# A fused Mamba-2 scan and gated feed-forward: the first eight groups of TensorE work put in another order

## The chip, the core and the metric

The kernel runs on one core of a Trainium2 chip. The core has a matrix engine (TensorE, PE in the profile; PEld is its loading of weights), VectorE (DVE), ScalarE (ACT), GpSimd (POOL) and the DMA queues that SyncE (SP) starts. Each engine works through its own list of instructions in the order in which the program gives them, and waits for other engines by semaphores. TensorE writes its sums into PSUM, which VectorE and ScalarE read; GpSimd works in the main on-chip memory alone. The metric is the time of one execution on the device in microseconds (us), as the median of several runs.

## The reference, cut to what matters

Two stages follow each other. The first is a linear recurrence over 768 tokens for 4 sequences of 8 heads; it is done in chunks, with a matrix of decays inside a chunk and a state between chunks. The second takes the result as 3072 tokens of 256 numbers and sends it through two matrices with h * cos(h) between them.

```python
# x: (4, 8, 768, 32)   a: (4, 8, 768)   B, C: (4, 8, 768, 16)
cum = np.cumsum(log(clip(a)), axis=-1)                       # within a chunk
L = np.exp(cum[..., :, None] - cum[..., None, :]) * causal   # decay from token j to token i
y = (einsum('bhin,bhjn->bhij', C, B) * L) @ x                # inside the chunk
y += einsum('bhin,bhnd->bhid', C, state) * np.exp(cum)       # from the chunks before
state = exp(sum(la)) * state + sum_j(B_j x_j decay_from_j)

h = y @ w_in                 # y as (3072, 256), w_in (256, 2048)
out = (h * np.cos(h)) @ w_out   # w_out (2048, 256)
```

## The kernel before

The kernel uses chunks of 128 tokens, six in all. The first of them, chunk 0, is cut into two units of 64 tokens for all four sequences, so that the feed-forward can begin early. For each unit `k` it does the following. `spread_a` copies the decay factors to all partitions by a matrix product; `decays0` turns them into the matrix of decays with a scan on VectorE (each value is the one before times a factor, plus a start value). `turn_b` and `turn_c` transpose B and C. `inner` makes C times B (the tile g), `weights` multiplies it by the decays, and `finish0` makes y and the sums for the state.

The PSUM has three kinds of buffers here: tag `h` with two banks, tag `o` with two banks, and pairs of banks:

```python
def bank(shape, name, tag):
    return psum.tile(shape, FP32, tag=tag, bufs=2, name=name)

def pair(name):
    return psum.tile([P, 2, 4 * P], FP32, tag="scan", bufs=2, name=name)

def spread_a(k, p, i=0, n=1, tag="o"):
    ps = (pair("a_ps")[:, 0] if tag is None else bank([P, 4 * P], "a_ps", tag))
    ...                                       # two matmuls into ps

def decays0(k, p, i=0, n=1):                  # scan over half i of n, for pair p of sequences
    ...
    V.tensor_tensor_scan(out=lams[k][:, p, hs].rearrange(flat),
                         data0=spread.pop((k, p, i)).rearrange(flat), ...)

def inner(k, t):
    gs[k, t] = g = pair("g")
    ...                                       # 16 small matmuls into g

def weights(k, q):                            # reads gs[k, q] and lams[k], writes units[k]
    ...
    V.tensor_tensor(out=m, in0=gs[k, q][...], in1=l, op=ALU.mult)
```

`finish0` takes one pair for unit 0 and two pairs for unit 1. Its first pair holds a part of y and also the sums for the state; it hands back `take`, which reads these sums:

```python
def finish0(k, between=None):
    m, xk = units[k], xrs[k]
    y = [pair("y") for _ in range(2)] if k else [pair("y")]
    ...   # k == 1: from the state into y; both: the state's sums into y[0][:, s, 3 * P:]; then m times x into y
    if between:
        between()
    if k:
        for t in range(2):
            ACT.copy(out=t_[:, t]..., in_=y[t][:, :, 0:P])
    else:
        ACT.copy(out=t_..., in_=y[0][:, :, 0:2 * P]...)

    def take():
        for t in range(2):
            ts = slice(t * D, (t + 1) * D)
            ACT.activation(new[:, :, :, ts], y[0][:, :, 3 * P:]..., AF.Copy, scale=slot[:, t:t + 1])
    ...
    return take, add
```

A step `n` of the feed-forward is 256 of the 2048 inner columns for a group of 256 tokens. `first` makes hp, `wind` takes the whole turns off it (ScalarE makes k, VectorE makes w), `gate` is the sine on ScalarE, `gated` multiplies on VectorE and is the last that reads hp, and `second` is the product with w_out. In chunk 0 the even steps belong to unit 0 and the odd ones to unit 1; the steps 0 and 1 need the same columns of w_in, and so do 2 and 3.

```python
def first(n, between=None):
    c, f = divmod(n, NF)
    hp[n] = bank([P, TB], "hp", "h")
    ...
    for e in range(2):
        for k in range(KT):
            PE.matmul(to_[:, e], lhsT=w_in[:, k, fs], rhs=y[:, k], start=(k == 0), stop=(k == KT - 1), ...)
        if between and e == 0:
            between()

def wind_k(n): ACT.activation(k, hp[n], AF.Copy, bias=0.25, scale=INV_2PI)
def wind_w(n): V.scalar_tensor_tensor(out=w, in0=hp[n], scalar=INV_2PI, in1=k, op0=ALU.mult, op1=ALU.subtract)
def gate(n):   ACT.activation(cos, cos, AF.Sin, bias=quarter, scale=TWO_PI)
def gated(n):  V.tensor_tensor(out=gT[n], in0=hp.pop(n), in1=cos, op=ALU.mult)
```

The weights come as 64-bit words and are made into 32-bit numbers in eight pieces for each matrix: `grade` is two passes on ScalarE and a clip on GpSimd, `join` two passes on VectorE and an add on GpSimd.

Of the kernel before, what the change touches and what calls it, by code (L numbers as in the profile page):

```python
# [25 lines left out]
def kernel(  # L26
# [17 lines left out]
    P = 128  # L44
# [4 lines left out]
    TB = NB * P  # L49
# [19 lines left out]
    def bank(shape, name, tag):  # L69
        return psum.tile(shape, FP32, tag=tag, bufs=2, name=name)  # L70
# [279 lines left out]
    def decays0(k, p, i=0, n=1):  # L350

        if p == i == 0:
            lams[k] = scan.tile([P, 2, H, W], FP32, tag="lam", bufs=4, name="lam")
        flat = "p h i -> p (h i)"
        hs = slice(i * H // n, (i + 1) * H // n)
        V.tensor_tensor_scan(out=lams[k][:, p, hs].rearrange(flat),
                             data0=spread.pop((k, p, i)).rearrange(flat),
                             data1=unit0[:, hs].rearrange(flat), initial=0.0,
                             op0=ALU.mult, op1=ALU.add)
# [12 lines left out]
    def turn_c():  # L372

        tp = bank([P, 4, P], "tp", "o")
        for r in range(4):
            PE.transpose(tp[:, r], c0[:, r].rearrange("p h n -> p (h n)"), ident)
        tp = tp.rearrange("p r (b k g) -> p k b g r", b=NB, k=2)

        def of(k, dst, **v):
            ACT.activation(dst.rearrange("p b (g r) -> p b g r", r=4), tp[:, k], AF.Copy, **v)  # L380

        def take(k):
            for t in range(2):
                of(k, cuts[k][:, t].rearrange("p q (s i) -> p (q s) i", s=2), scale=slot[:, t:t + 1])
        return take, of

    def turn_b(k, tp):

        for p in range(2):
            PE.transpose(tp[:, 2 * k + p], bs[:, k, p], ident)  # L390
        return lambda: ACT.copy(out=bTs[:, k], in_=tp[:, 2 * k:2 * k + 2])
# [32 lines left out]
        V.tensor_tensor(out=m, in0=gs[k, q][:, :, 0:2 * P].rearrange("p k (s i) -> p k s i", s=2),  # L424
                        in1=l, op=ALU.mult)

    def finish0(k, between=None):

        m, xk = units[k], xrs[k]
        y = [pair("y") for _ in range(2)] if k else [pair("y")]  # L430
        at_ = [[(y[t][:, s, p * W:(p + 1) * W] if k else
                 y[0][:, s, t * P + p * W:t * P + (p + 1) * W]) for p in range(2)]
               for t in range(2) for s in range(2)]
        if k:
            old = states0.pop(k)
            for p in range(2):
                for s in range(2):
                    for q in range(4):
                        r, c0 = slice(32 * q, 32 * q + 32), W * (q % 2)
                        PE.matmul(at_[2 * (q // 2) + s][p][c0:c0 + W], lhsT=old[r, s, p],  # L440
                                  rhs=rTs[k][r, 2 * p + s], start=(p == 0), stop=False,
                                  tile_position=(32 * q, c0), skip_group_check=True)
        sc = scs.pop(k).rearrange("p (q k h) n -> p q k (h n)", q=2, h=2)
        x2 = xk.rearrange("p q (k h) d -> p q k (h d)", h=2)
        for p in range(2):
            for s in range(2):
                ss = slice(s * W, (s + 1) * W)
                for q in range(4):
                    PE.matmul(y[0][32 * q:32 * q + 32, s, 3 * P + p * W:3 * P + (p + 1) * W],
                              lhsT=sc[ss, p, q], rhs=x2[ss, p, q], start=(k == p == 0), stop=True,  # L450
                              tile_position=(s * W, 32 * q), skip_group_check=True)
        for p in range(2):
            for t in range(2):
                for s in range(2):
                    ss = slice(s * W, (s + 1) * W)
                    for q in range(4):
                        PE.matmul(at_[2 * t + s][p][32 * q:32 * q + 32],
                                  lhsT=xk[ss, p, 4 * t + q], rhs=m[ss, p, 4 * t + q],
                                  start=False, stop=True,
                                  tile_position=(s * W, 32 * q), skip_group_check=True)  # L460
        if k == 0:
            yT[0] = two.tile([P, 2, 2, 2 * P], FP32, tag="yT", name="yT")
        t_ = yT[0][:, k]
        if between:
            between()
        if k:
            for t in range(2):
                ACT.copy(out=t_[:, t].rearrange("p (s i) -> p s i", s=2), in_=y[t][:, :, 0:P])
        else:
            ACT.copy(out=t_.rearrange("p t (s i) -> p s t i", s=2),  # L470
                     in_=y[0][:, :, 0:2 * P].rearrange("p s (t i) -> p s t i", t=2))
        states0[k + 1] = new = states.tile([P, 2, 2, 2 * D], FP32, tag="state0", bufs=2,
                                           name="state0")
# [4 lines that stand above are left out]
                ACT.activation(new[:, :, :, ts], y[0][:, :, 3 * P:].rearrange(  # L478
                    "p s (q d) -> p s q d", q=2)[:, :, :, ts], AF.Copy, scale=slot[:, t:t + 1])

        def add():
            dec = scan.tile([P, 2, 2, 2 * D], FP32, tag="whole", bufs=1, name="whole")
            r4 = reach1.rearrange("p (q s) i -> p s q i", s=2)
            for s in range(2):
                G.tensor_tensor(out=dec[:, s], in0=old[:, s],
                                in1=r4[:, s, :, W:].to_broadcast([P, 2, 2 * D]), op=ALU.mult)
            G.tensor_tensor(out=new, in0=new, in1=dec, op=ALU.add)
            for u in range(2):
                state[0, u] = new[:, u].rearrange("p s (t d) -> p s t d", t=2)
        return take, add  # L490
# [158 lines left out]
        c, f = divmod(n, NF)  # L649
        return (f % 2, f // 2) if c == 0 else divmod(f, NJ)  # L650

    def first(n, between=None):
        c, f = divmod(n, NF)
        hp[n] = bank([P, TB], "hp", "h")

        u, j = turn_of(n)
        if c == 0:
            to_, y = hp[n].rearrange("p (e i) -> p e i", e=2), yT[0][:, u]
        else:
            to_ = hp[n].rearrange("p (e t s i) -> p e t s i", e=2, t=2, s=2)  # L660
            y = yT[c].rearrange("p k (u s t i) -> p k u t s i", u=2, s=2, t=2)[:, :, u]
        for e in range(2):
            fs = slice((2 * j + e) * P, (2 * j + e + 1) * P)
            for k in range(KT):
                PE.matmul(to_[:, e], lhsT=w_in[:, k, fs], rhs=y[:, k],  # L665
                          start=(k == 0), stop=(k == KT - 1), skip_group_check=True)
            if between and e == 0:
                between()
# [16 lines left out]
    def gate(n):  # L685
        cos = turns[n]
        ACT.activation(cos, cos, AF.Sin, bias=quarter, scale=TWO_PI)  # L687
# [146 lines left out]
        decays0(0, p, i, 2)  # L834
    spread_a(0, 1, 1, 2, "h")
    decays0(0, 1, 1, 2)
    take_c, of_c = turn_c()
    tp_b = bank([P, 4, P], "tp", "o")
    take_b = turn_b(0, tp_b)
    take_c(0)  # L840
    take_b()
    scan_reach = reach0(1)
    scan_reach()
    weigh0(0)
    grade("in", 0)
    for t in range(2):
        inner(0, t)
    spread_a(1, 0, tag="h")
    for q in range(2):
        weights(0, q)  # L850
    take_c(1)
    join("in", 0)
    weigh_c(1, of_c)
    take_s0, _ = finish0(0)
    spread_a(1, 1, tag="o")
    take_b = turn_b(1, tp_b)
    take_b()
    inner(1, 0)
    for p in range(2):
        decays0(1, p)  # L860

    la = const.tile([RB, NU, P], FP32, name="la")
    cut = const.tile([RB, NU, P], FP32, name="cut")
# [62 lines left out]

    def first_steps():

        take_s0()
        first(0, lambda: inner(1, 1))  # L930
        weigh0(1)
        grade("in", 1)
        units_of_decay()
        for q in range(2):
            weights(1, q)
        take_s1, add_s1 = finish0(1, lambda: wind_k(0))
        join("in", 1)
        wind_w(0)
        first(1)
        rest = grade("out", 0, later=True)  # L940
        gate(0)
        rest()
        clips()
        gated(0)
        join("out", 0)
        wind(1)
        first(2)
        rest = grade("in", 2, later=True)
        gate(1)
        take_s1()  # L950
        rest()
        gated(1)
        second(0)
        grade("out", 1)
        join("in", 2)
        wind(2)
        first(3)
        rest = grade("in", 3, later=True)
        gate(2)
        join("out", 1)  # L960
        rest()
        gated(2)
        second(1)
        wind(3)
        rest = grade("out", 2, later=True)
        gate(3)
        join("in", 3)
        rest()
        gated(3)
        return add_s1  # L970

    add_s1 = first_steps()
# [86 lines left out]
```

## Time and profile before

The time is 375.29 us, the median of three runs (375.26 to 376.05). The span of the profiled execution is 373.6 us.

| what | measured |
|---|---|
| full scans of unit 1 on VectorE | 1.21 us at 11.59, 1.22 us at 12.98 |
| scans of unit 0 in four halves | 2.44 us in all, from 5.09 |
| y of unit 1 on TensorE | 17.08 to 18.87 us |
| hp 0 complete | about 17.1 us |
| second(0) starts on TensorE | 23.97 us |
| sine of step 0 on ScalarE | 19.88 us, 0.74 us long |
| take_s1 on ScalarE | 23.74 us, 0.61 us for both parts |
| one step's k, w, sine, gT in the stage behind | 0.60, 0.68, 0.72, 0.68 us |

How to read the rows of such a profile: a row of the timeline has the start in us, the length in us, the engine, the line of the kernel, the operation, the tile that is written, an arrow, the tiles that are read, the form, and how many instructions were merged into the row. In square brackets stands how long the engine had been idle, and what ended the wait. Rows of one engine can overlap a little[...].

### The profile page before, as it was taken

Reading aid. Unit: us, or ns where it says so; the run is one execution under the profiler, and the core shown is the slowest. Engines: PE = TensorE matmul, PEld = TensorE weight load, DVE = VectorE, ACT = ScalarE, POOL = GpSimd, SP = SyncE. Lnnn points to the kernel's source line nnn. Section 1 sums busy time; section 2 is a strip of 40 time slices with the busy share of each in tenths; the row PEclk is TensorE's granted clock in tenths of the full one; section 3 lists DMA queues with packets and bytes.
Section 4 is the critical chain, followed back from the end, with each engine's and each line's share of the span. In section 5 each row is a group of like instructions: output and inputs, shape, how many; then the busy total and the mean of one; then the engine's idle time right before and its main releaser. Section 6 shows DMA issues by size and latency. Waiting matters only on the chain.

```text
span 373.6 us, 8681 instructions
## 1 busy us (share of the span) xinstructions
PE 363.9 (97%) x3272; PEld 325.2 (87%) x3272; DVE 280.8 (75%) x470; ACT 172.6 (46%) x293; POOL 215.2 (58%) x334
## 2 busy tenths in 40 slices
PE   7989999999999999999999999999999999999995
PEld 4568887889889899998999999899999989999995
DVE  6859999889699957987858987766987872543653
ACT  3487756444344435344434435434434443444442
POOL 6576865589856347664454683453685343544451
PEclk9999999999999999999999999999999999999999
DMA  9988987315436641755122735121020000010011
GB/s 142 270 230 239 254 212 155 86 14 139 121 84 84 124 108 17 112 128 135 21 51 28 130 94 138 18 50 17 10 37 7 21 9 2 2 28 2 5 26 28
DMA packets 121353, 31.54 MB, mean 84 GB/s; under 512 B 90496, under 2 KB 117216, under 8 KB 121312
## 3 DMA queue, kind: packets, MB, share of 16 engines
q1 hardware_dynamic: 119024, 30.54, 38.1%
q10 hardware_dynamic: 2288, 0.46, 0.7%
q8 instruction: 26, 0.43, 0.5%
q14 instruction: 15, 0.12, 0.1%
HBM read 27.64 MB, written 3.34 MB: 83 GB/s over the span
## 4 chain that ended last, share of the span: by engine, by line
PE 72%; DVE 11%; POOL 6%; DMA 3%; issue 3%; SPq 2%; ACT 1%; POOLq 0%; DVEq 0%; ACTq 0%
PE hp L665 35%; PE o L774 30%; POOL words L711 3%; DMA xr<-in_x_dram 3%; PE y L604 2%; DVE mag L246 2%; DVE gT L692 2%; DVE w L678 2%; PE g L562 2%; DVE mag L244 1%; DVE lam L512 1%; POOL gd L717 1%; PE y L597 1%; DVE m L583 1%; POOL gd L719 1%
## 5 line engine op out<-in xcount | busy, mean ns | idle before, releaser
L665 PE MATMUL hp<-yT,w_in 128*128 128x256 f32 x768 | 184.1, 382 | 2.5 <-DVE gT L692 1.5
L665 PEld LDWEIGHTS hp<-yT,w_in 128*128 128x128 f32 x768 | 139.2, 190 | 22.8 <-issue 4.7
L717 POOL TENSOR_TENSOR gd<-gT 128x256 f32<-128x256 f32 x79 | 59.2, 750 | 99.0 <-DVE gT L692 85.3
L687 ACT ACTIVATE w<-w,quarter 128x512 f32<-128x512 f32 x96 | 69.2, 721 | 77.1 <-DVE w L678 77.1
L672 ACT ACTIVATE k<-hp 128x512 int32<-128x512 f32 x96 | 57.1, 595 | 83.1 <-PE hp L665 82.9
L678 DVE SCALAR_TENSOR_TENSOR w<-hp,k 128x512 f32<-128x512 f32 x96 | 65.5, 682 | 38.3 <-ACT k L672 37.9
L692 DVE TENSOR_TENSOR gT<-hp,w 128x512 f32<-128x512 f32 x96 | 65.3, 680 | 35.9 <-ACT w L687 27.1
L774 PE MATMUL o<-words,gd 128*128 128x128 f32 x474 | 65.8, 275 | 0.0
L774 PEld LDWEIGHTS o<-words,gd 128*128 128x128 f32 x474 | 59.3, 192 | 0.0
L512 DVE TENSOR_TENSOR_SCAN lam<-arow,unit 128x512 f32<-128x512 f32 x40 | 56.6, 1415 | 0.0
L774 PEld LDWEIGHTS o<-w_out,gT 128*128 128x128 f32 x316 | 47.5, 191 | 4.0
L720 POOL TENSOR_TENSOR gd<-gT,gd 128x128 f32<-128x128 f32 x79 | 44.6, 565 | 6.2
L774 PE MATMUL o<-w_out,gT 128*128 128x128 f32 x316 | 48.0, 274 | 0.0
L719 POOL TENSOR_TENSOR gd<-gT,gd 128x128 f32<-128x128 f32 x79 | 44.2, 559 | 6.2
L583 DVE TENSOR_TENSOR m<-g,lam 128x256 f32<-128x256 f32 x80 | 30.9, 415 | 0.5
L774 PE MATMUL o<-w_out,gd 128*128 128x128 f32 x158 | 30.6, 275 | 0.0
L774 PE MATMUL o<-words,gT 128*128 128x128 f32 x158 | 30.6, 275 | 0.0
L736 PE MATMUL o<-w_out,gT 128*128 128x256 f32 x128 | 30.3, 380 | 0.0
L736 PEld LDWEIGHTS o<-w_out,gT 128*128 128x128 f32 x128 | 24.2, 190 | 3.4 <-POOL w_out L254 0.2
L774 PEld LDWEIGHTS o<-w_out,gd 128*128 128x128 f32 x158 | 24.0, 192 | 0.0
L774 PEld LDWEIGHTS o<-words,gT 128*128 128x128 f32 x158 | 24.0, 192 | 0.0
L791 DVE TENSOR_TENSOR sum<-ps,sum 128x256 f32<-128x256 f32 (+1 forms) x27 | 16.7, 645 | 0.6
(108 smaller groups left out, 264.4 us busy)
## 6 DMA issues: line engine op xcount, KB each, us to landing
arow<-a_cut SPq DMA_DIRECT2D x20, 512.0 KB
words<-in_moe_w_in_dram SPq DMA_DIRECT2D x8, 512.0 KB
words<-in_moe_w_out_dram SPq DMA_DIRECT2D x8, 512.0 KB
out_dram<-sum SPq DMA_DIRECT2D x18, 128.0 KB
blocks<-in_B_dram SPq DMA_DIRECT2D x128, 8.0 KB
blocks<-in_C_dram SPq DMA_DIRECT2D x128, 8.0 KB
xr<-in_x_dram SPq DMA_DIRECT2D x14, 128.0 KB
along<-a_all SPq DMA_DIRECT2D x20, 64.0 KB
```

The source lines that it names most:

```text
L512: V.tensor_tensor_scan(out=lam[c, b][:, hs].rearrange("p h i -> p (h i)"), data0=rows_.rearrange("p h i -> p (h i)"), data1=unit[:, b % 2 ...
L583: V.tensor_tensor(out=m_[js, :, :, is_], in0=g_[js, :, :, is_], in1=l_[js, :, :, is_], op=ALU.mult)
L665: PE.matmul(to_[:, e], lhsT=w_in[:, k, fs], rhs=y[:, k], start=(k == 0), stop=(k == KT - 1), skip_group_check=True)
L672: ACT.activation(k, hp[n], AF.Copy, bias=0.25, scale=INV_2PI)
L678: V.scalar_tensor_tensor(out=w, in0=hp[n], scalar=INV_2PI, in1=k, op0=ALU.mult, op1=ALU.subtract)
L687: ACT.activation(cos, cos, AF.Sin, bias=quarter, scale=TWO_PI)
L692: V.tensor_tensor(out=gT[n], in0=hp.pop(n), in1=cos, op=ALU.mult)
L717: G.tensor_tensor(out=d[:, 0:2], in0=g[:, 1:2].to_broadcast([P, 2, P]), in1=g[:, 3::-3], op=ALU.subtract)
L719: G.tensor_tensor(out=d[:, 2], in0=g[:, 0], in1=d[:, 0], op=ALU.subtract)
L720: G.tensor_tensor(out=d[:, 3], in0=g[:, 2], in1=d[:, 2], op=ALU.subtract)
L736: PE.matmul(o[c, u][:, t], lhsT=g[:, 2 * e + t], rhs=w_out[:, 2 * j + e], start=(j == e == t == 0), stop=(j == NJ - 1 and e == 1), skip_gr ...
L774: PE.matmul(at[q], lhsT=a_[q], rhs=w[q], start=(j == 0 and q in starts), stop=(j == NJ - 1), skip_group_check=True)
```

## The change

The change puts the work of chunk 0 into another order; the arithmetic stays the same. The first half of unit 1's decays is scanned in two halves, straight behind the scans of unit 0, where VectorE waits for the first g; the scan for the reach (how much of the state is left at each token) moves back behind the rest. Both halves of `inner` of unit 1 come ahead of hp 0, and `finish0(1)` goes into hp 0, between its two halves. The steps 2 and 3 take their hp from the pairs in place of tag `h`, and come ahead of `second(0)`; `second(0)` and `second(1)` move back. `take_s1` moves from behind `gate(1)` to behind `gate(3)`. `clips` (the decays of the later chunks) goes ahead of `gate(0)`, and `join` goes ahead of `gated` in the steps 0 and 1. It is meant to keep TensorE fed over the first steps, in which the hp banks and the waits for y hold it up.

```diff
@@ -424,7 +424,7 @@
         V.tensor_tensor(out=m, in0=gs[k, q][:, :, 0:2 * P].rearrange("p k (s i) -> p k s i", s=2),
                         in1=l, op=ALU.mult)
 
-    def finish0(k, between=None):
+    def finish0(k):
 
         m, xk = units[k], xrs[k]
         y = [pair("y") for _ in range(2)] if k else [pair("y")]
@@ -461,8 +461,6 @@
         if k == 0:
             yT[0] = two.tile([P, 2, 2, 2 * P], FP32, tag="yT", name="yT")
         t_ = yT[0][:, k]
-        if between:
-            between()
         if k:
             for t in range(2):
                 ACT.copy(out=t_[:, t].rearrange("p (s i) -> p s i", s=2), in_=y[t][:, :, 0:P])
@@ -649,9 +647,9 @@
         c, f = divmod(n, NF)
         return (f % 2, f // 2) if c == 0 else divmod(f, NJ)
 
-    def first(n, between=None):
+    def first(n, between=None, tag="h"):
         c, f = divmod(n, NF)
-        hp[n] = bank([P, TB], "hp", "h")
+        hp[n] = bank([P, TB], "hp", tag) if tag else pair("hp")[:, 0]
 
         u, j = turn_of(n)
         if c == 0:
@@ -834,30 +832,34 @@
         decays0(0, p, i, 2)
     spread_a(0, 1, 1, 2, "h")
     decays0(0, 1, 1, 2)
+    spread_a(1, 0, 0, 2, None)
+    decays0(1, 0, 0, 2)
     take_c, of_c = turn_c()
     tp_b = bank([P, 4, P], "tp", "o")
     take_b = turn_b(0, tp_b)
+    spread_a(1, 0, 1, 2, "h")
+    decays0(1, 0, 1, 2)
     take_c(0)
     take_b()
-    scan_reach = reach0(1)
-    scan_reach()
     weigh0(0)
     grade("in", 0)
     for t in range(2):
         inner(0, t)
-    spread_a(1, 0, tag="h")
+    spread_a(1, 1, tag="h")
     for q in range(2):
         weights(0, q)
     take_c(1)
     join("in", 0)
+    decays0(1, 1)
+    take_s0, _ = finish0(0)
+    take_b = turn_b(1, tp_b)
+    scan_reach = reach0(1)
+    scan_reach()
+    take_b()
+    take_s0()
+    for t in range(2):
+        inner(1, t)
     weigh_c(1, of_c)
-    take_s0, _ = finish0(0)
-    spread_a(1, 1, tag="o")
-    take_b = turn_b(1, tp_b)
-    take_b()
-    inner(1, 0)
-    for p in range(2):
-        decays0(1, p)
 
     la = const.tile([RB, NU, P], FP32, name="la")
     cut = const.tile([RB, NU, P], FP32, name="cut")
@@ -926,47 +928,47 @@
 
     def first_steps():
 
-        take_s0()
-        first(0, lambda: inner(1, 1))
         weigh0(1)
         grade("in", 1)
         units_of_decay()
         for q in range(2):
             weights(1, q)
-        take_s1, add_s1 = finish0(1, lambda: wind_k(0))
+        states_of = []
+        first(0, lambda: states_of.extend(finish0(1)))
+        take_s1, add_s1 = states_of
         join("in", 1)
-        wind_w(0)
+        wind(0)
         first(1)
         rest = grade("out", 0, later=True)
+        clips()
         gate(0)
         rest()
-        clips()
+        join("out", 0)
         gated(0)
-        join("out", 0)
+        first(2, tag=None)
         wind(1)
-        first(2)
         rest = grade("in", 2, later=True)
         gate(1)
+        rest()
+        join("in", 2)
+        gated(1)
+        first(3, tag=None)
+        wind(2)
+        rest = grade("out", 1, later=True)
+        gate(2)
+        rest()
+        join("out", 1)
+        second(0)
+        gated(2)
+        wind(3)
+        second(1)
+        rest = grade("in", 3, later=True)
+        gate(3)
         take_s1()
         rest()
-        gated(1)
-        second(0)
-        grade("out", 1)
-        join("in", 2)
-        wind(2)
-        first(3)
-        rest = grade("in", 3, later=True)
-        gate(2)
-        join("out", 1)
-        rest()
-        gated(2)
-        second(1)
-        wind(3)
-        rest = grade("out", 2, later=True)
-        gate(3)
         join("in", 3)
-        rest()
         gated(3)
+        grade("out", 2)
         return add_s1
 
     add_s1 = first_steps()
```

## The prediction

> **What bounds the kernel now.** I read the page first (engine shares, slices, chain), then the PE timeline of the first 31 us with what PE waited for, then VectorE over the same stretch, and last the busy shares of the stage behind it.
>
> ```profile
> PE 363.9 (97%) x3272; PEld 325.2 (87%) x3272; DVE 280.8 (75%) x470; ACT 172.6 (46%) x293; POOL 215.2 (58%) x334
> ...
> PE   7989999999999999999999999999999999999995
> ...
> DVE  6859999889699957987858987766987872543653
> ...
> PEclk9999999999999999999999999999999999999999
> ...
> PE hp L665 35%; PE o L774 30%; POOL words L711 3%; DMA xr<-in_x_dram 3%; PE y L604 2%; DVE mag L246 2%; DVE gT L692 2%; DVE w L678 2%; PE g L562 2%; DVE mag L244 1%; DVE lam L512 1%; POOL gd L717 1%; PE y L597 1%; DVE m L583 1%; POOL gd L719 1%
> ```
>
> PE is full from the first slices on. The whole idle time of PE is 373.6 - 363.9 = 9.7 us, so a change in the head can bring very little; it can lose more, because nothing behind it has slack to take a delay back.
>
> ```profile
> 13.76 0.67 PE L415 MATMUL g<-cT,turned 32*64 32x128 f32 x16 [0.46 <-ACT turned L391]
> 14.36 1.13 PE L665 MATMUL hp<-yT,w_in 128*128 128x256 f32 x4
> 15.42 0.67 PE L415 MATMUL g<-cT,turned 32*64 32x128 f32 x16
> 16.02 1.13 PE L665 MATMUL hp<-yT,w_in 128*128 128x256 f32 x4
> 17.08 0.69 PE L440 MATMUL y<-rT,state 32*64 32x64 f32 x32
> ...
> 19.20 1.99 PE L665 MATMUL hp<-yT,w_in 128*128 128x256 f32 x8 [0.33 <-ACT yT L468]
> 21.49 1.32 PE L665 MATMUL hp<-yT,w_in 128*128 128x256 f32 x5 [0.30 <-DVE gT L692]
> ...
> 25.77 1.89 PE L665 MATMUL hp<-yT,w_in 128*128 128x256 f32 x8
> ```
>
> These are the steps to be moved: g of unit 1 in two halves around half of hp 0, y of unit 1 at 17.08, hp 1 at 19.20, hp 2 at 21.49 (it waits for gated(0), which frees its bank), hp 3 at 25.77. Full groups of eight follow each other at 1.73 us from 29.54 on (33.07, 34.80, 36.52), which is 0.216 us for one pass of 256 columns.
>
> ```profile
> 8.16 0.70 DVE L398 TENSOR_TENSOR_SCAN m<-a_ps,m 128x260 f32<-128x260 f32 x1 [0.64 <-PE a_ps L396]
> 9.32 1.29 DVE L424 TENSOR_TENSOR m<-g,lam 128x512 f32<-128x512 f32 x2 [0.46 <-PE g L415]
> ...
> 16.15 0.69 DVE L424 TENSOR_TENSOR m<-g,lam 128x512 f32<-128x512 f32 x1 [0.96 <-PE g L415]
> ...
> 20.65 0.69 DVE L692 TENSOR_TENSOR gT<-hp,w 128x512 f32<-128x512 f32 x1 [2.15 <-ACT w L687]
> ...
> 28.72 0.68 DVE L692 TENSOR_TENSOR gT<-hp,w 128x512 f32<-128x512 f32 x1
> ```
>
> VectorE's gap is the one around 8.16; gT 0 ends at 21.3, gT 2 only at 29.4. Then the stage that follows:
>
> ```profile
> 29.50:53.90 24.40, 24.36 (x113) 21.24 (x113) 23.79 (x32) 16.63 (x29) 18.32 (x19) 1.00 0.89 248
> ```
>
> Columns: length, then busy time of PE, PEld, DVE, ACT, POOL. PE and VectorE are both full (24.36 and 23.79 of 24.40 us). A PE that is ahead at 29.5 us would meet VectorE; a PE that is behind takes VectorE with it, since each step's w waits for its hp.
>
> ```profile
> 1.06 2.93 PE L84 MATMUL warm<-ones 128*128 128x512 f32 x4 [1.06 <-DVE quarter L277]
> 3.92 2.34 PE L346 MATMUL a_ps<-m,those 128*64 128x256 f32 x16
> ```
>
> **What the Trainium skill says.** "TensorE: Matmul & The Clock Gate", section "HAM oscillation": no PE gaps of over about 3.4 us, or PE falls back to half its clock. The trace shows the cold half: the warm-up has two passes of 512 and two of 256 columns, 2 x 0.432 + 2 x 0.216 = 1.30 us at the later pace, and took 2.93; the granted-clock row doesn't show it. "PSUM — Partial Sum Buffer", section "Specifications (TRN2)": eight banks of 2 KiB, 512 FP32 each. The kernel spends all eight: tag h two, tag o two, and two pair tiles of two banks. Section "Engine vs sequencer instructions" there: ScalarE, VectorE and GpSimd are strict FIFO. The traces agree: the rows on each engine follow the program's order. So I place the instructions of each engine in the new program order and carry durations over from the rows.
>
> **Part 1: the first scan of unit 1 earlier.** Removed: two full scans of 1.21 us at 11.59 and 12.98. Added: two halves of about 0.61 us at 7.5 and 8.6, one full scan behind join("in", 0); the reach scan (0.70) goes from 8.16 to behind that. VectorE has about 1.7 us between scan end (7.5) and weights(0) (9.32), and two halves are 1.2, so weights(0) moves by 0.1 us at most, and finish0(0) waits for x at 10.82 anyway. VectorE: join to 11.7, full scan to 12.9, reach to 13.55. PE no longer has spread_a(1,1) (1.08 us at 11.85) behind y 0: turn_b and reach by about 12.9. ACT: yT 0 to 12.6, take_b to 12.92, take_s0 to 13.5. So g of unit 1: first half 12.97 to 13.64, second (its pair is released by take_s0) 13.6 to 14.27; weights(1) 13.7 to 15.0, against 16.84 before: 1.8 us won here.
>
> **Part 2: y of unit 1 inside hp 0.** Half of hp 0 at 14.05 (0.87 us of issue), y from 15.05 (it needs weights(1) for its second pair), as long as before, 17.08 to 18.87 = 1.79, so to 16.84; the other half of hp 0 16.7 to 17.6 lies under the yT copies (ACT 16.9 to 17.55). hp 1 from 17.6 instead of 19.20: 1.6 us earlier. The price: hp 0 is complete at 17.75 instead of 17.1, so k 0 runs 17.8 to 18.4 (was 17.18), w 0 to 19.1, sine to 19.85. join("out", 0) and clips now come ahead of gated(0): gT 0 at 20.75 against 20.65.
>
> **Part 3: hp 2 and hp 3 in pair tiles.** hp 2 needs no gated(0) any more: a pair is free after the second yT copy (17.5), w_in's piece 1 is added by 18.35; so it runs 19.33 to 21.1, against 21.49 to 24.1. For hp 3 I read which pairs are live. There are two. y[0] of unit 1 also holds the sums for the state, which take_s1 reads, and take_s1 is moved behind gate(3). gate(3) needs hp 3. So y[0]'s pair can't be hp 3's, the only other pair is hp 2's, and hp 3 must wait until gated(2) has read hp 2. That hp 3 uses only one bank of a pair doesn't help, if a tile is given back as a whole.
>
> When is gated(2)? ACT, VectorE and GpSimd make it, in program order:
> - GpSimd: clip of out 0 19.0 to 19.6, clips to 20.65, add of out 0 20.85 to 22.1 (1.27), clip of in 2 to 22.75.
> - VectorE: gT 0 to 21.35, w 1 to 21.95, join("in", 2) 22.8 to 24.0, gT 1 to 24.65, w 2 to 25.2.
> - ACT: k 1 20.4, sine 1 22.0 to 22.7, k 2 23.25 to 23.85, sine 2 25.25 to 25.95.
> - GpSimd: add of in 2 24.05 to 25.3, clip of out 1 to 25.95; VectorE join("out", 1) 26.0 to 27.2, gT 2 27.2 to 27.9 (before 28.72 to 29.4).
>
> So hp 3 starts at 27.95, and second(0) and second(1) stand behind it in PE's order: PE stands still from 21.1 to 27.95, 6.85 us. Then four groups at 1.73: hp 3, second(0), second(1), hp 4 end at 34.9, plus 0.25 until the last sum is there; w 4 then starts about 35.7 on VectorE (k 4 is 0.6) against 32.17 before: +3.5 us. An idle time of 6.85 us is also long enough for the half clock; the warm-up lost 2.93 - 1.30 = 1.6 us to it, and I take the same: +1.6. Sum +5.1 at 30 to 37 us, and since PE and VectorE are both full behind it, all of it reaches the end: 375.3 + 5.1 = 380.4. I take 0.2 off for short waits that a later stage may swallow: 380.2.
>
> **Rivals.** (A) hp 3 has its bank after all (half a pair is enough, or y[0] comes free by other means). Then hp 3 runs 21.1 to 22.9, second(0) to 24.6, second(1) after gT 1 to 26.4, hp 4 to 28.2, where before it started at 29.54. But ACT, VectorE and GpSimd keep their chain: gT 2 27.9, then w 3, join("in", 3) behind the add of out 1, gT 3 31.1, w 4 at 31.0 to 31.7 against 32.17. VectorE is full until 58 us, where hp already waits 0.4 us for gT, so only VectorE's 0.5 to 1.1 us counts: about 374.4. For it speaks the name of the change, which means both banks to be used; against it the place of take_s1. I give it 15%. (B) The stall is there but PE stays warm or is cold only briefly: +3.5, 378.8; against it, the idle time is far over the skill's 3.4 us and the start shows the cold pace. (C) The moves of parts 1 and 2 come to nothing because x or the words arrive late: x of unit 1 is needed at 15.6 instead of 17.7. The row for in 1 shows its words there by 14.12, and x of unit 1 is the next in the queue, so at most some tenths. In all three the rest of the program is the same; only the head's shift differs.
>
> **Range and chances.** With the stall (85%) the time lies between 378 and 382.5, by how long the half clock lasts (none to 3 us) and by errors of half a microsecond in the chain to gated(2); without it about 374.4. The range 376.0 to 382.5 leaves out the second and the worst tail. 2% is 7.5 us: faster than 367.8 would need almost all of PE's idle time, 1%; slower than 382.8 needs a long cold stretch, 8%; within 2%: 91%.
>
> **What would show it.** In the trace after: (1) a full-width scan fewer at 12 to 14 us, two half scans at 7.5 to 9.3, weights(0) still at 9.3 to 9.4; (2) both g halves by 14.3, y of unit 1 near 15.1, hp 1 near 17.6; (3) hp 2 near 19.3 without a wait for gT; (4) hp 3 with the one long wait of PE, 6 to 7 us, put down to VectorE's gT, and its passes near 0.43 instead of 0.216 us; (5) from 40 us on the same rows, about 5 us later. Wrong would be: hp 3 close behind hp 2 (then rival A), or a long wait with passes at 0.216 us (rival B).

## The result and the profile after

The changed kernel takes 381.91 us (median of four runs, 381.57 to 382.39) against 375.29 us. The ratio is 1.0173, with a 95% interval of 1.0154 to 1.0191: 6.6 us slower.

From the page of the changed kernel, in the order of the lines shown of the kernel before: busy times, the slices, and the chain of waits by line.

```profile
PE 366.1 (96%) x3276; PEld 327.9 (86%) x3276; DVE 280.3 (74%) x471; ACT 172.6 (45%) x293; POOL 215.0 (56%) x334
...
PE   8929999999999999999999999999999999999996
...
DVE  7672899989979966987775887875888782554543
...
PEclk9996999999999999999999999999999999999999
...
PE hp L663 37%; PE o L772 30%; SPq L110 4%; PE y L602 3%; PE o L734 2%; PE g L560 2%; POOL words L709 2%; DMA bc<-in_C_dram 1%; PE y L595 1%; DMA arow<-a_cut 1%; DVE mag L246 1%; DVE gT L690 1%; DVE w L676 1%; DVE mag L244 1%; POOL gd L715 1%
```

The span is 380.6 us, 7.0 longer. There are two marks of it: the third slice of PE (19 to 28.5 us) has a 2 where the kernel before has an 8, and the slice behind it (28.5 to 38 us) was granted 6 tenths of the clock. PE's busy time is 2.2 us longer although the work is the same (3276 matmuls in place of 3272, since one spread is cut in halves): it has slow passes, shown below.

The PE timeline of the changed kernel, the same steps as before:

```profile
12.49 1.19 PE L415 MATMUL g<-cT,turned 32*64 32x128 f32 x32 [0.17 <-ACT turned L391]
13.61 1.13 PE L663 MATMUL hp<-yT,w_in 128*128 128x256 f32 x4
14.67 0.45 PE L440 MATMUL y<-rT,state 32*64 32x64 f32 x14
15.58 0.50 PE L440 MATMUL y<-rT,state 32*64 32x64 f32 x18 [0.45 <-issue]
...
17.11 3.07 PE L663 MATMUL hp<-yT,w_in 128*128 128x256 f32 x13
21.99 1.67 PE L663 MATMUL hp<-yT,w_in 128*128 128x256 f32 x7 [1.80 <-issue]
28.82 3.75 PE L663 MATMUL hp<-yT,w_in 128*128 128x256 f32 x8 [5.16 <-DVE gT L690]
32.37 4.85 PE L734 MATMUL o<-w_out,gT 128*128 128x256 f32 x16
37.05 1.89 PE L663 MATMUL hp<-yT,w_in 128*128 128x256 f32 x8
```

The row at 17.11 holds the second half of hp 0 (4 passes), all of hp 1 (8) and the first pass of hp 2. The row at 28.82 is hp 3. It waited 5.16 us, and the profile names gT on VectorE as what ended the wait. Its 8 passes take until second(0) starts at 32.37, 3.55 us in place of 1.73, and the two groups behind it take 4.68 in place of 3.46. hp 4 starts at 37.05; before, it started at 29.54.

VectorE in the changed kernel: weights(0), weights(1), gT 2, w 3, w 4.

```profile
9.12 1.29 DVE L424 TENSOR_TENSOR m<-g,lam 128x512 f32<-128x512 f32 x2 [0.39 <-PE g L415]
...
13.22 1.29 DVE L424 TENSOR_TENSOR m<-g,lam 128x512 f32<-128x512 f32 x2
...
27.99 0.68 DVE L690 TENSOR_TENSOR gT<-hp,w 128x512 f32<-128x512 f32 x1
33.30 0.69 DVE L676 SCALAR_TENSOR_TENSOR w<-hp,k 128x512 f32<-128x512 f32 x1 [4.63 <-ACT k L670]
...
39.61 0.69 DVE L676 SCALAR_TENSOR_TENSOR w<-hp,k 128x512 f32<-128x512 f32 x1 [3.29 <-ACT k L670]
```

gT 2 ends at 28.67 and hp 3 starts at 28.82. In the kernel before, w 4 stood at 32.17; here it is at 39.61, 7.4 us later, after two long waits of VectorE for PE. The busy shares by stages of the changed kernel (length; busy PE, PEld, DVE, ACT, POOL; granted clock; DMA share; GB/s):

```profile
25.00:30.00 5.00, 1.18 (x3) 1.03 (x4) 2.81 (x5) 1.27 (x2) 3.11 (x3) 0.80 0.75 181
30.00:35.00 5.00, 5.00 (x14) 3.96 (x13) 1.12 (x2) 2.13 (x5) 0.61 (x1) 0.51 1.07 305
35.00:40.00 5.00, 5.00 (x25) 4.41 (x24) 1.68 (x3) 2.98 (x6) 1.86 (x2) 1.00 0.58 138
```

In the first stretch every engine stands for a good part: PE is busy for 1.18 of 5 us, VectorE for 2.81. In the next PE is "busy" for 5.00 of 5 us but does 14 passes where 24 or 25 are usual, at a granted clock of 0.51.

### The profile page after: what moved, and what is told of

The parts are those of the page before. It is cut to its first block, busy times and chain, and to the rows that moved or that the text cites. A ratio compares the mean times of both kernels' runs of the same rounds, so it can differ in the third digit from the quotient of the medians.

```text
span 380.6 us, 8692 instructions
## 1 busy us (share of the span) xinstructions
PE 366.1 (96%) x3276; PEld 327.9 (86%) x3276; DVE 280.3 (74%) x471; ACT 172.6 (45%) x293; POOL 215.0 (56%) x334
## 4 chain that ended last, share of the span: by engine, by line
PE 78%; SPq 5%; DVE 5%; POOL 5%; DMA 3%; issue 2%; ACT 1%; POOLq 0%; ACTq 0%
PE hp L663 37%; PE o L772 30%; SPq L110 4%; PE y L602 3%; PE o L734 2%; PE g L560 2%; POOL words L709 2%; DMA bc<-in_C_dram 1%; PE y L595 1%; DMA arow<-a_cut 1%; DVE mag L246 1%; DVE gT L690 1%; DVE w L676 1%; DVE mag L244 1%; POOL gd L715 1%
## 5 line engine op out<-in xcount | busy, mean ns | idle before, releaser
L772 PEld LDWEIGHTS o<-w_out,gT 128*128 128x128 f32 x316 | 47.5, 191 | 4.0
L734 PE MATMUL o<-w_out,gT 128*128 128x256 f32 x128 | 31.3, 390 | 0.0
L734 PEld LDWEIGHTS o<-w_out,gT 128*128 128x128 f32 x128 | 25.3, 198 | 3.7
L232 POOL TENSOR_SCALAR mag<-mag 128x512 f32<-128x512 f32 x16 | 11.6, 726 | 11.1 <-ACT mag L231 11.0
```

The costliest lines, as they stand in the source:

```text
L734: PE.matmul(o[c, u][:, t], lhsT=g[:, 2 * e + t], rhs=w_out[:, 2 * j + e], start=(j == e == t == 0), stop=(j == NJ - 1 and e == 1), skip_gr ...
L772: PE.matmul(at[q], lhsT=a_[q], rhs=w[q], start=(j == 0 and q in starts), stop=(j == NJ - 1), skip_group_check=True)
```

## The experiments

My theory: y[0] of unit 1 keeps its pair until take_s1; hp 3 therefore gets the pair of hp 2 and has to wait for gated(2); PE cools in that wait. All edits are against the changed kernel unless the text says otherwise. The kernel before ran beside each group of runs: 375.37 us beside runs 1 to 4, 375.5 beside runs 6 to 9, 375.14 beside runs 5, 10 and 11.

### 1. hp 3 in a bank of tag h

```diff
-        first(3, tag=None)
+        first(3)
```

> Only hp of step 3 goes back to a bank of tag h. Theory (the pair of y[0] is held by take_s1, so hp 3 must wait for gated(2), and PE cools meanwhile): hp 3 follows hp 2 at about 23.7 us with no long wait, its passes stay at 0.216 us, hp 4 starts near 28.8 and the time is 374.3 to 375.3, some 7 us under the changed kernel. Rival 1 (the loss comes from unit 1's new order or from the joins ahead of gated): the time stays at 380 to 382. Rival 2 (second(0) and second(1) come too late, whatever bank hp 3 has): 378 to 380.

Measured: 375.88 us, ratio to the kernel before 1.001 (0.9998 to 1.0022). The PE timeline of this run:

```profile
16.99 3.07 PE L663 MATMUL hp<-yT,w_in 128*128 128x256 f32 x13
21.85 3.40 PE L663 MATMUL hp<-yT,w_in 128*128 128x256 f32 x15 [1.79 <-issue]
25.09 3.62 PE L734 MATMUL o<-w_out,gT 128*128 128x256 f32 x16
28.54 1.89 PE L663 MATMUL hp<-yT,w_in 128*128 128x256 f32 x8
```

hp 3 follows hp 2 in one row, at 0.216 us for a pass. One word in one line takes the whole loss away, so both rivals fall. The time is 0.6 us above the span I gave; runs 8 to 11 are about that.

### 2. hp 3 in a pair, take_s1 early

```diff
         take_s1, add_s1 = states_of
+        take_s1()
...
         gate(3)
-        take_s1()
```

> hp 3 stays in a pair, but take_s1 comes straight behind the copies of y of unit 1. Theory: y[0]'s pair is free at about 18.4 us, hp 3 takes it without a wait, and the time is that of the run with hp 3 in tag h within 0.5 us (374.3 to 375.5). If a pair is held for another reason than take_s1, hp 3 still waits for gT 2 at about 28.8 and the time is 381 to 382.

Measured: 375.8 us, ratio 1.0009 (0.9993 to 1.0024), the same as run 1. hp 2 and hp 3 again run in one row, 21.98 to 25.38. So a pair serves hp 3 as well as a bank of tag h does, and the place of take_s1 alone decides whether it is free.

### 3. The wait left in, PE kept at work

```diff
+        fill(bank([P, 4, P], "warm", "o"), 5)
         first(3, tag=None)
```

> The wait of hp 3 stays; five products of ones with 512 columns each, into a free bank, fill 4.3 us of it, so that PE doesn't stand idle for 5.2 us. Theory (the slow passes of hp 3 and second(0) come from the idle time): the passes of hp 3 are at 0.216 us, hp 3 and second(0) take 3.46 us in place of about 6.5, and the time is 3 us under the changed kernel, 378.5 to 379.3. If the half clock has another cause, the time stays at 381.5 to 382.3.

Measured: 379.65 us, ratio 1.0111 (1.0077 to 1.0146). The fills (`warm` in the rows) only write a bank that is free at the time. Its PE timeline:

```profile
23.70 4.46 PE L84 MATMUL warm<-ones 128*128 128x512 f32 x10
29.04 1.97 PE L663 MATMUL hp<-yT,w_in 128*128 128x256 f32 x8 [0.88 <-DVE gT L690]
30.84 3.62 PE L734 MATMUL o<-w_out,gT 128*128 128x256 f32 x16
34.30 1.89 PE L663 MATMUL hp<-yT,w_in 128*128 128x256 f32 x8
```

hp 3 still waits for gT 2 and starts 0.2 us later than in the changed kernel, but hp 4 starts at 34.30 in place of 37.05. From hp 3 to hp 4 it is 5.26 us here and 8.23 (37.05 - 28.82) there. The idle time thus costs 2.97 us of slow passes on top of the wait itself; in the medians the difference is 2.3 us (381.91 - 379.65), under the 3 us I gave, and the time lies 0.35 above the span of 378.5 to 379.3.

### 4. and 5. Each part alone

Run 4 keeps unit 1's new order and gives the steps 0 to 3 their old order and banks. Run 5 is the kernel before with only the steps 0 to 3 as changed.

```diff
# run 4, the core of it
-        first(2, tag=None)
+        first(2)
...
-        first(3, tag=None)
+        second(0)
+        grade("out", 1)
...
+        first(3)
```

> Unit 1's new order (scans, g, y inside hp 0) with the old order of the steps 0 to 3 and their banks. Theory: no long wait; hp 1 ends 0.8 us earlier than before, but k 0 is 1.1 us later than before, and hp 2 waits for gT 0; the time is 374.5 to 376.0, near the kernel before. Rival 1 (unit 1's new order makes the loss): 379 to 382.

```diff
# run 5, against the kernel before, the core of it
+        first(2, tag=None)
...
-        first(2)
...
+        first(3, tag=None)
...
-        second(0)
-        grade("out", 1)
...
-        first(3)
```

> The complement: unit 1 in the old order, and only the steps 0 to 3 as changed (hp 2 and hp 3 in pairs, take_s1 behind gate(3), joins ahead of gated). Theory (the whole loss is in the bank of hp 3): hp 3 waits 4 to 6 us for gT 2, passes at half pace behind it, time 381.0 to 383.0. Rival (the loss needs unit 1's new order too): under 379.

Measured: run 4 375.69 us, ratio 1.0013 (0.9995 to 1.0031); run 5 381.79 us, ratio 1.0176 (1.0163 to 1.0189). The PE timeline of run 5:

```profile
28.70 3.75 PE L665 MATMUL hp<-yT,w_in 128*128 128x256 f32 x8 [5.20 <-DVE gT L692]
32.25 4.86 PE L736 MATMUL o<-w_out,gT 128*128 128x256 f32 x16
36.95 1.89 PE L665 MATMUL hp<-yT,w_in 128*128 128x256 f32 x8
```

These are the rows of the changed kernel at 28.82, 32.37 and 37.05 within 0.12 us. The steps' part makes the whole loss; unit 1's part makes no difference that can be told from none.

### 6. and 7. What is the gap in hp 2?

The wait of 1.80 us at 20.2 to 22 us is put down to "issue". Counted from the first matmul on, it stands behind 347 records (a record is one matmul in the trace) in both kernels. Run 6 starts two loads of weights later, run 7 cuts the warm-up into more and shorter matmuls; both have hp 3 in tag h. Each was executed once.

```diff
# run 6
-    for w in (("in", 2), ("out", 1), ("in", 3), ("out", 2), ("in", 4)):
+    for w in (("in", 2), ("out", 1), ("in", 3)):
...      # at the end of clips()
+        for w in (("out", 2), ("in", 4)):
+            fetch(*w)
```

> Hp of step 3 in tag h, and two of the 512 KB loads of weights (out 2 and in 4) start only behind the clips, at about 21.5 us. The gap of PE at 20.1 to 21.9 us, which the profile puts down to issue, comes behind the same 347th matmul record in the kernel before, in the changed one and in three of the four runs. Theory (it waits for its next block of instructions, and that transfer stands behind the loads of the weights): with 1 MB less in the queues before 21 us the gap falls from 1.8 us to under 1.0. Rival (the fetch takes its 6 us whatever else moves): the gap stays at 1.6 to 1.9.

```diff
# run 7
-    fill(bank([P, 4, P], "warm", "o"), 1)
-    fill(bank([P, 2, P], "warm", "o"), 1)
+    for blocks_ in (4, 2):
+        warm = bank([P, blocks_, P], "warm", "o")
+        for i in range(blocks_):
+            fill(warm[:, i:i + 1])
```

> Hp of step 3 in tag h, and the two warm-up products cut into six of 128 columns, which is 8 matmul records more ahead of everything else with the same columns. Theory (a block of instructions ends there): the gap stays behind the 347th record, which is now the first pass of hp 1 instead of the first of hp 2, and the gap on y moves by 8 records as well. Rival (something that hp 2 needs comes late, w_in's piece 1 or its bank): the gap stays in front of hp 2's second pass.

PE in run 6, then PE in run 7:

```profile
22.16 5.08 PE L663 MATMUL hp<-yT,w_in 128*128 128x256 f32 x15 [2.06 <-issue]
```

```profile
17.38 1.56 PE L663 MATMUL hp<-yT,w_in 128*128 128x256 f32 x6
22.57 6.70 PE L663 MATMUL hp<-yT,w_in 128*128 128x256 f32 x22 [3.63 <-issue]
```

Run 7: with 8 records more at the head the gap comes 7 passes sooner (behind 6 passes of hp, not 13), which is behind 348 recorded matmuls. The gap on y, which was to move as well, is not seen in run 7. The gap here is 1.8 us longer and ends at 22.57, where that of run 1 ends at 21.85. So it belongs to a count of instructions and to a time, not to hp 2 or to what hp 2 reads. A matmul record goes with one weight load; the gap of 0.45 us on y in the changed kernel stands behind 220 records, and 347 - 220 = 127 pairs are 254 instructions. The Trainium skill, "Runtime: NRT & Kernel Launch", section "Instruction fetch mechanics", says that an engine refills its instruction memory in blocks of 16 KiB, 256 instructions, "mostly hidden". The block fits; "hidden" doesn't hold here, where the gap in hp was 0.3 to 3.6 us.

The traces also have the transfer itself. Of 19 to 20 us in the changed kernel:

```profile
q8 instruction: 1, 0.02, 6.9%
```

This is one packet of 16 KB in the instruction queue, in flight from 19.58 to 20.69 us; the gap ends at 21.99. The whole execution has 26 such packets. At 256 instructions each, as that page has it, they hold 6656 (an estimate); PE ran 6552 matmuls and weight loads, and no other engine more than 471 instructions. In all 13 profiles the second of these packets lands between 20.50 and 21.91 us, and the gap ends 1.2 to 1.5 us behind its landing (run 7: 21.17 and 22.57; run 11: 21.05 and 22.48). The first lands at 14.29 in the changed kernel, and the gap on y ends at 15.58. So the gap is a wait for the next block of instructions; what takes the 1.2 to 1.5 us behind the landing is not shown.

Run 6 missed: the gap stayed at 2.06 us. DMA traffic in 15 to 20 us fell only from 376 GB/s (run 1) to 319, and the packet started no sooner (19.83, in run 1 19.39). From 20 to 22 us it fell to under 50 GB/s, and the packet took 1.07 us all the same, 1.11 in run 1. What decides when it starts is not shown. Its time of 379.73 us, and 378.16 us in run 7, are each of one execution and are not compared; 15 passes after run 6's gap took 4.92 us (22.16 to 27.08) where run 1 took 3.24.

### 8. to 11. Why is nothing gained when the stall is gone?

In run 1 hp 4 starts at 28.54, 1.0 us sooner than before, and the time is no better. Four runs look for that microsecond; all have hp 3 in tag h. Run 8 moves take_s1 and the grading of out 2 on ScalarE. Run 9 grades and joins each piece a step earlier (in 1 is piece 1 of w_in, out 0 piece 0 of w_out). Run 10 has the gradings and joins where the kernel before has them. Run 11 is run 10 with two spreads whole in place of halves, 8 records fewer.

```diff
# run 8
         take_s1, add_s1 = states_of
+        take_s1()
...
         gate(3)
-        take_s1()
...
         gated(3)
-        grade("out", 2)
...      # in the loop, behind wind(n)
+            if n == AHEAD:
+                grade("out", 2)
```

> Hp of step 3 in tag h, take_s1 early and the grading of out 2 behind k 4 on ScalarE, nothing else. Theory: k 4 follows hp 4 at 30.5 instead of 32.0, but gT 3 still ends at 31.7 on VectorE, so w 4 starts at 31.7 to 31.9 against 32.65, and the time is 374.8 to 375.3, 0.6 to 1.0 under the run with hp 3 in tag h alone. Rival (ScalarE's order doesn't matter here): 375.6 to 376.2.

```diff
# run 9, the core of it
         grade("in", 1)
+        grade("out", 0)
...
         join("in", 1)
+        join("out", 0)
...
         gated(0)
+        join("in", 2)
```

> Hp of step 3 in tag h, and each piece of the weights is graded and joined one step earlier, behind gated of the step before, so that VectorE and GpSimd don't wait for each other between 15 and 31 us. Theory (with the stall gone, the head's gain is lost because w 4 on VectorE starts no earlier than before, and VectorE is full from there to 58 us): w 4 starts at about 31.1 against 32.2 before and the time is 374.1 to 374.9. Rival (the chunk 0 stage is bound by PE alone, and hp 4 at 28.5 should have shown already): no further gain, 375.4 to 376.2.

```diff
# run 10, the core of it
+        take_s1()
...
-        join("out", 0)
         gated(0)
+        join("out", 0)
...
-        join("in", 2)
         gated(1)
-        first(3, tag=None)
+        first(3)
+        grade("out", 1)
+        join("in", 2)
```

> Unit 1's new order, hp 2 in a pair and hp 3 in tag h ahead of second(0), take_s1 early, but the grading and joining of the weights at the places where the kernel before has them. Theory (in the run with hp 3 in tag h, VectorE lost 2.8 us waiting for GpSimd's clips between 23 and 30 us, since join stands ahead of gated in each step): gT 3 ends near 30.2 in place of 31.75, w 4 starts at 31.1 to 31.5 against 32.65 there and 32.2 before, and the time is 374.2 to 375.0. Rival (the stage up to 58 us takes what it takes): 375.4 to 376.2.

```diff
# run 11, against run 10
-    spread_a(0, 1, 0, 2, "h")
...
+    spread_a(0, 1, tag="h")
...
-    spread_a(1, 0, 0, 2, None)
...
+    spread_a(1, 0, tag="h")
```

> The run before with 8 matmul records fewer at the head: two of the spreads whole in place of halves. Theory of the instruction blocks: the gap stays behind the 347th record, now the first pass of hp 3 in place of hp 2, and it still ends at about 22 us, so hp 2 is complete near 21 instead of 23.7; the time is 373.9 to 375.0. Rival: the gap stays in front of hp 2's second pass.

| run | us | ratio to the kernel before (95%) | w 4 starts |
|---|---|---|---|
| 8 | 376.07 | 1.0002 (0.9978 to 1.0026) | 32.03 |
| 9 | 377.66 | 1.0051 (1.0034 to 1.0067) | 34.11 |
| 10 | 375.41 | 1.0014 (1.0003 to 1.0025) | 32.08 |
| 11 | 375.86 | 1.0019 (1.001 to 1.0028) | 32.03 |

All four missed the gain I expected. Run 10 shows best why. The busy shares by stages, first of the kernel before, then of run 10, and PE's row for hp 12 in run 10:

```profile
25.00:30.00 5.00, 4.85 (x23) 3.98 (x22) 4.11 (x8) 4.47 (x8) 3.83 (x4) 1.00 0.59 139
30.00:35.00 5.00, 5.00 (x24) 4.39 (x24) 4.81 (x8) 3.78 (x6) 3.75 (x5) 1.00 1.12 344
```

```profile
25.00:30.00 5.00, 5.00 (x25) 4.38 (x24) 4.93 (x7) 3.98 (x8) 3.66 (x4) 1.00 0.69 168
30.00:35.00 5.00, 5.00 (x25) 4.37 (x24) 4.93 (x9) 4.32 (x8) 3.75 (x5) 1.00 1.14 317
```

```profile
58.34 1.97 PE L663 MATMUL hp<-yT,w_in 128*128 128x256 f32 x8 [0.39 <-DVE gT L690]
```

VectorE is now busy for 4.93 of 5 us from 25 us on, five microseconds sooner than it was full in the kernel before. w 4 stands at 32.08 all the same (32.17 before). The rows of VectorE, first of the kernel before, then of run 10:

```profile
25.08 0.69 DVE L246 SCALAR_TENSOR_TENSOR mag<-words,mag 128x512 uint32<-128x512 uint32 x1
26.59 0.69 DVE L678 SCALAR_TENSOR_TENSOR w<-hp,k 128x512 f32<-128x512 f32 x1 [0.82 <-ACT k L672]
27.20 0.58 DVE L244 TENSOR_SCALAR mag<-mag 128x512 uint32<-128x512 uint32 x1
```

```profile
25.10 1.14 DVE L246 SCALAR_TENSOR_TENSOR mag<-words,mag 128x512 uint32<-128x512 uint32 x1
...
26.77 1.12 DVE L244 TENSOR_SCALAR mag<-mag 128x512 uint32<-128x512 uint32 x1
```

The wait of 0.82 us for k 2 is gone, but two operations of its joins took 0.99 us longer (0.45 and 0.54); GpSimd was at work at the time of both (from 25.09 and from 26.33). And hp 12 waits for VectorE at 58.34, where it stood at 58.41 before. PE ahead of VectorE is worth nothing here; the rival I wrote down for run 10 ("takes what it takes") is right.

Run 9 went wrong in another place. ScalarE and PE of run 9:

```profile
16.71 0.67 ACT L231 ACTIVATE mag<-words 128x512 f32<-128x512 f32 x1 [1.97 <-DMA words<-in_moe_w_out_dram]
```

```profile
20.82 0.48 PE L663 MATMUL hp<-yT,w_in 128*128 128x256 f32 x1 [0.57 <-POOL w_in L254]
23.27 4.93 PE L663 MATMUL hp<-yT,w_in 128*128 128x256 f32 x15 [1.97 <-issue]
```

The words of out 0 land at 16.7 us, and grading them ahead of the yT copies held those up (17.86 against 16.96 in run 1); in 1 was joined too late for hp 2, the block of instructions came later, and the passes behind were slow. w 4 is 2.0 us later than in run 10, and so is the end: run 9 is 2.2 us above the kernel before, run 10 0.3.

Run 11 confirms the count once more. Its PE timeline:

```profile
17.32 4.58 PE L663 MATMUL hp<-yT,w_in 128*128 128x256 f32 x20
22.48 1.99 PE L663 MATMUL hp<-yT,w_in 128*128 128x256 f32 x8 [0.58 <-PE hp L663]
```

With 8 records fewer the gap stands in front of hp 3, behind 346 records, and ends at 22.48; hp 2 is complete before it. The profile puts this one down to hp, not to issue, but what hp 3 needs was ready by 21.3 us (gT 0 ends at 21.28). hp 12 still starts at 58.30. No version tried beats the kernel before.

## Why the prediction was right, point by point

- **The stall of hp 3** (part 3, the main step) was right, and is shown: runs 1 and 2 remove it by one line each from two sides, run 5 makes it alone. The cause is as the prediction put it: the pair of y[0], held by take_s1, behind a gate that needs hp 3.
- **Its start** was given as 27.95; it was 28.82. gT 2 was to end at 27.9 and ended at 28.67. The chain ran late from its first link: hp 0 was to be complete at 17.75 and k 0 ran at 18.28. The gap of 0.45 us on y, of which the prediction knew nothing, is part of it.
- **The length of the wait** was given as 6.85 us and was 5.16: hp 3 came 0.87 us later, but hp 2 ended at about 23.7 and not at 21.1, mostly for the gap of 1.80 us. This step (hp 2 from 19.33 to 21.1) failed. It cost nothing here, since hp 3 was not free to start anyway.
- **The half clock** was right as a mechanism and mis-sized: +1.6 us from the warm-up, measured 2.97 (run 3). The clock granted in single microseconds is 0.50 from 29 to 34 us and 0.57 in the next, so about 6 us of PE's work ran at half pace; a loss of 1.6 us stands for about 3. Rival B, which let PE stay warm, is out. The sentence that the granted-clock row doesn't show it holds only for the warm-up, where the row says 1.00; in the stall it shows 0.80 and 0.51. That the warm-up's 2.93 us are the same half clock is therefore not shown.
- **The sum.** Two terms are off: hp 3 later by 0.87 us and the slow passes dearer by 1.37. That is 2.2 us, and w 4 is at 39.61 where the prediction's sum gives 37.3. What was taken off for later stages was 0.2; 7.4 us at w 4 became 7.0 in the span. So the time came out 1.7 us above the 380.2 named, inside the range.
- **Parts 1 and 2** were right in order and close in time: weights(0) at 9.12 (9.3 to 9.4 given), both halves of g by 13.7 (14.3), y at 14.67 (15.05), hp 1 at about 17.98, four passes after 17.11 (17.6). What they win is lost again: run 4 stands at 1.0013.
- **Rival A** named the value of the change without the stall: 374.4, from 0.5 to 1.1 us that VectorE would gain. Measured 375.8 to 375.9 (runs 1 and 2), which is no gain. Its reason, that PE ahead at 29.5 us would meet VectorE, is what run 10 shows; the half microsecond for VectorE was too much.

## What to carry to other kernels

A buffer is free when its last reader is done, not when its main one is: before giving a pair to a new tile, list for each live tile the last instruction that reads any part of it, and where that instruction stands in its engine's order. If it stands behind something that needs the new tile, the new tile will wait for another buffer. And before moving work of the engine that looks full, look at the stage behind: here a lead that met a second full engine brought nothing, while a delay was passed on almost whole (7.4 us at w 4, 7.0 in the span).

## What the runs showed of the hardware that was not expected

TensorE ran into a gap at a fixed count of instructions: behind 346 to 348 recorded matmuls in all 13 profiles, whatever stood there, and it ended between 21.85 and 23.32 us, 1.2 to 1.5 us behind the landing of a packet of instructions. Moving the count by 8 records up or down (runs 7 and 11) moved the gap with it.

The clock fell after shorter idle times than the 3.4 us of the Trainium skill, "TensorE: Matmul & The Clock Gate", section "HAM oscillation". Run 6 was idle for 2.06 us, run 8 for 2.15 us at the same place. The windows of 20 to 25 us, first of run 6, then of run 8:

```profile
20.00:25.00 5.00, 2.94 (x8) 2.27 (x7) 3.72 (x7) 3.14 (x6) 3.28 (x7) 0.72 0.53 112
```

```profile
20.00:25.00 5.00, 2.85 (x14) 2.35 (x14) 3.38 (x6) 4.21 (x8) 3.56 (x6) 1.00 0.83 225
```

The first was granted 0.72 of the clock and did 8 passes, the second 1.00 and 14. The mean granted clock of each execution on record agrees: in runs 1, 2, 4 and 8 to 10, whose profiles have TensorE idle for 1.6 to 2.5 us there, 20 of 102 executions had a mean of 0.995 or less; of the 19 of run 11, idle for 0.6 us, none had, and of 115 of the kernel before, idle for 0.8 us, 2. What decides in the single case these runs do not show; a gap of 2 us is not safe.
